# Windowed attention in front of two expert layers: the plain heads' value shift moved from a VectorE copy to a DMA inside SBUF, and half of the other value copies put on ScalarE

## The chip, the core and the metric

One core of one Trainium2 chip runs the whole program. It has TensorE (PE), VectorE (DVE), ScalarE (ACT), GpSimd (POOL), and SyncE (SP), which here only issues transfers. SP, ScalarE and GpSimd each have a queue of transfers, all of which run on the core's 16 DMA engines. The metric is the time of one execution on the device, in microseconds (us); less is better. L12 is line 12 of the kernel.

## The reference

Attention over 4 batches of 8 heads, 576 positions of 64 numbers each; a position sees the 32 positions up to its own (heads 0 to 3, "plain") or every fourth of the last 128 (heads 4 to 7, "dilated"). Its output goes through a layer that sends each of 2304 tokens to one of 8 experts, and then through a second layer.

```python
scores = scale * np.matmul(q, k.transpose(0, 1, 3, 2))
mask_plain = (rel >= 0) & (rel < 32)
mask_dil = (rel >= 0) & (rel < 128) & (rel % 4 == 0)
attn = exp(scores - max) / (sum + 1e-09)       # masked, h < 4 plain, else dilated
x = np.matmul(attn, v)                         # then tokens x 512
idx = np.argmax(xn @ en.T / tau, axis=1)       # expert of each token
y[e] = gate * (np.maximum(x[e] @ w1[e], 0) @ w2[e])
out = (h - np.tanh(h)) @ w_out                 # h = y @ w_in
```

## The kernel before

The first 180 us or so are the attention and the choice of experts; the expert layer and the last layer follow, and the change doesn't touch these two.

**Units and turns.** The attention is cut into 19 units (`units`), numbered 0 to 18. A unit is ("d", b, c) for half of the dilated heads of batch b, ("p", b, c) for half of the rows of the plain heads, ("l", 0, c) and ("t", 0, 0) for the rests of 576 positions that don't fill 128 rows. Units 9 and 11 are plain ones of batch 2, units 14 and 17 plain ones of batch 3, units 15 and 16 are "l". The order is written out by hand and each engine runs it in order. Turn n of the loop does, one after the other:

- `plan[n]`: transfers that are issued ahead, nearly all on SP (`load`, L420);
- `scores(n + 2)` on TensorE, and between its halves the transposes of the keys and queries of unit n + 3 (L550); then `softmax(n + 2)`: VectorE takes the maximum `mx` (L666) and subtracts it into `sm` (L669), ScalarE makes the exponentials `pr` (L674);
- `mid[n]`;
- `values(n)` on TensorE (L722), and after it the transposes of the probabilities of unit n + 1, copied out by ScalarE as `pT` (L685); VectorE divides the result (L731 to L742);
- `after[n]`.

The scores lie in one PSUM buffer (`sc`), so TensorE can't begin the scores of unit n + 3 (L631) before `sm` of unit n + 2 has read it. `mid` and `after` hold the extra work: `route_norm`, `route_low`, `route_transpose` (a transposing transfer on SP, L919), `route_choice` (TensorE's products L953, then small operations), `route_place`, which build the expert choice group by group of tokens, and the value copies below.

**Values.** A block of 32 queries needs the values of its own 32 keys and of the 32 before, on 64 partitions for each of two heads. For the plain heads `load_vp(b, par)` brings the own blocks into partitions 32 to 63 (par 0) or 96 to 127 (par 1) of `vwp[b % 2]`, and `shift_vp(b, par)` copies them one block further into the 32 partitions below, which makes them "the block before". It runs in `after` of turns 0 and 1 (batch 0), 2 and 3, 6 and 7, 10 and 11 (batch 3), eight times in all. For the dilated heads `expand_v` copies pieces of 32 partitions into `vwd` and `vwl`, through `vcopy`, which gives every VP-th copy to ScalarE and the others to VectorE.

**Semaphores of transfers.** The transfers that SP and ScalarE issue take eight semaphores, DMAHW0 to DMAHW7, in turn in the program's order, whichever of the two issues them. Each waits before it is issued until the last transfer that took its own semaphore has landed. SP's queue is issued in order.

Of the kernel before, what the change touches and what calls it, by code (L numbers as in the profile page):

```python
# [49 lines left out]
T0 = R0 * KAPPA - T1 * T1  # L50
BURST = 10
NST = 6
VP = 3


@with_exitstack
def kernel(
# [18 lines left out]
    nc = tc.nc  # L76
# [317 lines left out]
    with ExitStack() as actx:  # L394
# [18 lines left out]
        def four(src, b, h0, i0, n):  # L413
            return src[b, h0:h0 + 4, 4 * i0:4 * i0 + 4 * n, :].rearrange("h (i c) d -> i h (c d)", c=4)
# [53 lines left out]
        vwp = [tp.tile([128, 18, 2, D + 1], F32, tag=f"vwp{i}", name=f"vwp{i}", bufs=1) for i in range(2)]  # L468
# [32 lines left out]
        def shift_vp(b, par):  # L501

            p0 = 64 * par
            nc.vector.tensor_copy(out=vwp[b % 2][p0:p0 + 32, 1:18], in_=vwp[b % 2][p0 + 32:p0 + 64, 0:17])

        ncopy = [0]

        def vcopy(o, i):
            ncopy[0] += 1
            (nc.scalar.copy if ncopy[0] % VP == 0 else nc.vector.tensor_copy)(out=o, in_=i)  # L510

# [588 lines left out]
        for b in range(B):  # L1100
            plan[max(at["p", b, 0] - 1, 0)].append((room_x, (b,)))
            plan[(3, 7, 11, 14)[b]].append((load_x, (b,)))
            if b:
                for g in range(4):
                    after[4 * b - 4 + (3 * g) // 3].append((expand_v, (b, g)))
            for par in range(2):
                after[(0, 2, 6, 10)[b] + par].append((shift_vp, (b, par)))
            after[at["p", b, 0]].append((keep_vt, (b,)))
# [31 lines left out]
        for c in range(2):  # L1140
            for nm, src, eng in (("k", k, nc.sync), ("q", q, nc.scalar)):
                eng.dma_start(
                    out=raw["d", nm, 0][:, :, 128 * c:128 * c + 128],
                    in_=four(src, 0, 4, 0, 128)[:, :, 128 * c:128 * c + 128],
# [93 lines left out]
    for x in x2l[::-1] + x2h[::-1]:  # L1238
# [10 lines left out]
        out=key, in0=ncnt[0:1, :], scalar=float(E), in1=later, op0=ALU.mult, op1=ALU.add  # L1249
    )  # L1250
    nc.vector.scalar_tensor_tensor(
        out=key, in0=is_first, scalar=float(E * (NT + 1)), in1=key, op0=ALU.mult, op1=ALU.add
# [3 lines left out]
        out=ahead, in0=key.unsqueeze(1).to_broadcast(sh), in1=key.unsqueeze(2).to_broadcast(sh), op=ALU.is_gt  # L1256
# [6 lines left out]
        out=at_place, in0=rank.unsqueeze(1).to_broadcast(sh), in1=order.unsqueeze(2).to_broadcast(sh), op=ALU.is_equal  # L1263
# [4 lines left out]
        out=picked[:, 0:E], in0=at_place, in1=order.unsqueeze(1).to_broadcast(sh), op=ALU.mult  # L1268
# [8 lines left out]
        out=before, in0=rank.unsqueeze(1).to_broadcast(sh), in1=order.unsqueeze(2).to_broadcast(sh), op=ALU.is_lt  # L1277
# [11 lines left out]
        out=zf[:, 0:E], in0=sums[:, 0:E], scalar=float(XS), in1=pn, op0=ALU.mult, op1=ALU.add  # L1289
    )  # L1290
    nc.vector.scalar_tensor_tensor(
        out=zf[:, E:2 * E], in0=pn, scalar=-16.0, in1=caps, op0=ALU.add, op1=ALU.is_lt
    )
    nc.vector.scalar_tensor_tensor(
        out=zf[:, 2 * E:], in0=zf[:, 0:E], scalar=-float(E * XS), in1=zf[:, E:2 * E], op0=ALU.add, op1=ALU.mult
# [8 lines left out]
        out=mine, in0=rank.unsqueeze(2).to_broadcast(sh), in1=order.unsqueeze(1).to_broadcast(sh), op=ALU.is_equal  # L1304
# [465 lines left out]
```

## Time and profile before

| what | value |
|---|---|
| runs shown | 784.86, 784.91, 788.17 us; median 784.91 |
| profiled execution | 786.13 us; span from first to last instruction 784.5 us |
| mean granted clock of TensorE | 0.948 |
| busy over the span | PE 92%, DVE 62%, ACT 49%, POOL 26% |

The span is what the views of the trace count from; 1.6 us of the profiled execution lie outside it. A wait in brackets, as [1.28 <-DVE vwp L504], is the idle time of the engine before the instruction and what ended it. PEclk of 1.00 is the full clock of TensorE, 0.50 half of it. A chain of work that ended last can be followed back only to 172 us in this trace, so in the attention the waits are read engine by engine.

### The profile page before, as it was taken

Reading aid. Unit: us, or ns where it says so; the run is one execution under the profiler, and the core shown is the slowest. Engines: PE = TensorE matmul, PEld = TensorE weight load, DVE = VectorE, ACT = ScalarE, POOL = GpSimd, SP = SyncE. Lnnn points to the kernel's source line nnn. Section 1 sums busy time; section 2 is a strip of 40 time slices with the busy share of each in tenths; the row PEclk is TensorE's granted clock in tenths of the full one; section 3 lists DMA queues with packets and bytes.
Section 4 is the critical chain, followed back from the end, with each engine's and each line's share of the span. In section 5 each row is a group of like instructions: output and inputs, shape, how many; then the busy total and the mean of one; then the engine's idle time right before and its main releaser. Section 6 shows DMA issues by size and latency. Waiting matters only on the chain.

```text
span 784.5 us, 16969 instructions
## 1 busy us (share of the span) xinstructions
PE 718.1 (92%) x6773; PEld 451.9 (58%) x6773; DVE 486.3 (62%) x1019; ACT 381.5 (49%) x812; POOL 200.3 (26%) x244
## 2 busy tenths in 40 slices
PE   8787898538999999999997999999999999999994
PEld 5666676425666666788854555555555555555541
DVE  4788597585777777989869997333334343424420
ACT  4565547333655656777556565332423332423401
POOL 2155526375000000000003221412321322322311
PEclk9998698658999999999999999999999999999998
DMA  9869757749988868998600410100100100100001
GB/s 225 176 165 220 167 130 170 217 178 291 256 246 241 252 215 204 276 268 257 230 29 28 109 54 1 41 1 1 41 0 1 41 1 1 41 0 1 22 22 43
DMA packets 115828, 95.33 MB, mean 122 GB/s; under 512 B 72187, under 2 KB 99099, under 8 KB 115739
## 3 DMA queue, kind: packets, MB, share of 16 engines
q1 hardware_dynamic: 109083, 77.12, 36.9%
q0 software_dynamic: 5312, 16.40, 6.3%
q8 instruction: 55, 0.90, 0.5%
q10 hardware_dynamic: 1344, 0.62, 0.3%
q14 instruction: 34, 0.28, 0.1%
HBM read 67.12 MB, written 18.26 MB: 109 GB/s over the span
## 4 chain that ended last, share of the span: by engine, by line
PE 63%; DVE 5%; issue 4%; ACT 3%; POOL 1%; DMA 1%; POOLq 0%; SPq 0%; ACTq 0%; DVEq 0%
PE hp L1543 21%; PE po L1599 20%; PE y L1368 11%; PE ph L1348 10%; DVE w2l L187 1%; ACT w2h L177 1%; ACT sq L1406 1%; DVE c L1585 1%; POOL out L1608 1%; DMA xTe<-xs 1%; ACT u L1553 0%; DVE c L1563 0%; ACT U L1575 0%; POOL gl L1581 0%; DVE y L1427 0%
## 5 line engine op out<-in xcount | busy, mean ns | idle before, releaser
L1556 DVE CUSTOM_DVE_ANT_0 U<-u,sig 128x384 f32<-128x384 f32 x96 | 52.1, 580 | 161.2 <-ACT u L1553 161.2
L1581 POOL TENSOR_TENSOR gl<-c,gh 128x768 f16<-128x768 f32 x48 | 83.0, 1730 | 259.5 <-ACT gh L1580 259.5
L1553 ACT ACTIVATE u<-hp 128x384 f32<-128x384 f32 x96 | 46.0, 485 | 176.2 <-PE hp L1543 169.0
L1543 PE MATMUL hp<-x2h,win_h 128*128 128x384 f16 x384 | 125.2, 326 | 5.7 <-DVE c L1563 4.4
L1543 PE MATMUL hp<-x2h,win_l 128*128 128x384 f16 x384 | 125.2, 326 | 0.0
L1543 PE MATMUL hp<-x2l,win_h 128*128 128x384 f16 x384 | 124.0, 326 | 0.0
L1348 PE MATMUL ph<-xTe,w1h 128*128 128x352 f16 (+6 forms) x512 | 102.7, 294 | 10.3 <-DMA xTe<-xs 8.3
L1543 PEld LDWEIGHTS <-win_h 128*128 128x128 f16 x768 | 75.1, 98 | 59.5 <-DVE c L1563 7.6
L1599 PE MATMUL po<-wo_l,gh 128*128 128x512 f16 x288 | 109.2, 379 | 0.0
L1599 PE MATMUL po<-wo_h,gl 128*128 128x512 f16 x288 | 109.2, 379 | 0.0
L1599 PE MATMUL po<-wo_h,gh 128*128 128x512 f16 x288 | 109.1, 379 | 0.0
L1599 PEld LDWEIGHTS <-gh 128*128 128x128 f16 x576 | 56.3, 98 | 64.5 <-issue 1.0
L1348 PE MATMUL ph<-xTe,w1l 128*128 128x352 f16 (+6 forms) x256 | 75.3, 294 | 0.0
L1368 PE MATMUL y<-hh,w2h 128*128 128x352 f16 (+6 forms) x256 | 74.7, 292 | 0.0
L1368 PE MATMUL y<-hh,w2l 128*128 128x352 f16 (+6 forms) x256 | 74.6, 291 | 0.0
L1368 PE MATMUL y<-hl,w2h 128*128 128x352 f16 (+6 forms) x256 | 74.6, 291 | 0.0
L1348 PEld LDWEIGHTS <-w1h 128*128 128x128 f16 x512 | 50.5, 99 | 25.3 <-issue 9.2
L1368 PEld LDWEIGHTS <-w2h 128*128 128x128 f16 x512 | 50.1, 98 | 17.2 <-issue 0.8
L1585 DVE SCALAR_TENSOR_TENSOR c<-U,c 128x768 f32<-128x768 f32 x48 | 45.9, 957 | 11.2 <-ACT U L1575 11.2
L1543 PEld LDWEIGHTS <-win_l 128*128 128x128 f16 x384 | 37.6, 98 | 26.4
L1448 POOL DMA_DIRECT2D row_d<-rw x8 | 4.3, 534 | 174.0 <-ACT rw L1447 174.0
L1599 PEld LDWEIGHTS <-gl 128*128 128x128 f16 x288 | 28.2, 98 | 34.0
(278 smaller groups left out, 1251.7 us busy)
## 6 DMA issues: line engine op xcount, KB each, us to landing
wst<-in_moe_w SPq DMA_DIRECT2D x64, 512.0 KB, 7.6
wst<-in_moe_w_in SPq DMA_DIRECT2D x16, 512.0 KB, 5.6
wst<-in_moe_w_out SPq DMA_DIRECT2D x16, 512.0 KB, 3.6
vwp<-in_v SPq DMA_DIRECT2D x16, 144.0 KB, 6.2
rv<-in_v SPq DMA_DIRECT2D x4, 512.0 KB
rk<-in_k SPq DMA_DIRECT2D x16, 128.0 KB, 3.5
rq<-in_q SPq DMA_DIRECT2D x16, 128.0 KB, 5.2
xp<-xd_d SPq DMA_DIRECT2D x4, 512.0 KB, 4.2
```

What stands on the lines that cost most here:

```text
L177: nc.scalar.activation(out=hi, in_=st, func=ACTF.Copy, scale=SW)
L187: nc.vector.scalar_tensor_tensor(out=lo, in0=st, scalar=SW, in1=hi, op0=ALU.mult, op1=ALU.subtract)
L1348: nc.tensor.matmul(ph[:, 0:CAPS[e]], lhsT=wt[e, f // 2][w][:, c:c + 128], rhs=xT[:, a + d, 0:CAPS[e]], start=(i == 0), stop=(i == 11), ski ...
L1368: nc.tensor.matmul(y[dc][:, 0:CAPS[e]], lhsT=w[:, c:c + 128], rhs=h[:, f, 0:CAPS[e]], start=(f == 0 and i == 0), stop=(f == 7 and i == 2), ...
L1406: nc.scalar.activation(out=st["sq"][:, dc, 0:n], in_=y[dc][:, 0:n], func=ACTF.Square)
L1543: early(b, "x2", nc.tensor.matmul(hp[:, a, 0:NB], lhsT=w[d][:, 128 * f:128 * f + 128], rhs=x[d][:, c0:c0 + NB], start=(w is win_h and x is ...
L1553: nc.scalar.activation(out=u[:, a], in_=hv[:, a], func=ACTF.Square, accum_out=usum[:, n:n + 1])
L1556: early(b, "sg", nc.vector.tensor_tensor_reduce(out=U[:, a], in0=u[:, a], in1=sig2[:, c0:c0 + NB], scale=1.0, scalar=0.0, op0=ALU.mult, op ...
L1581: nc.gpsimd.tensor_tensor(out=gl, in0=tc_, in1=gh, op=ALU.subtract)
L1585: nc.vector.scalar_tensor_tensor(out=c, in0=U, scalar=T0, in1=c, op0=ALU.add, op1=ALU.mult)
L1599: nc.tensor.matmul(po[t][:], lhsT=g[:, a, 128 * t:128 * t + 128], rhs=w, start=(f == 0 and i == 0), stop=(f == 15 and i == 2), skip_group_ ...
L1608: i = nc.gpsimd.indirect_dma_start(out=out, out_offset=bass.IndirectOffsetOnAxis(ap=tok["id"][:, T:T + 1], axis=0), in_=o[:], in_offset=No ...
```

## The change

`shift_vp` issues a DMA on ScalarE's queue from SBUF to SBUF, for the same 32 partitions of 2210 numbers (8840 bytes each), in place of a copy on VectorE. VP goes from 3 to 2, so that of the 88 value copies of `vcopy` 44 are on ScalarE, before 29.

```diff
-VP = 3
+VP = 2
...
         def shift_vp(b, par):
 
             p0 = 64 * par
-            nc.vector.tensor_copy(out=vwp[b % 2][p0:p0 + 32, 1:18], in_=vwp[b % 2][p0 + 32:p0 + 64, 0:17])
+            nc.scalar.dma_start(out=vwp[b % 2][p0:p0 + 32, 1:18], in_=vwp[b % 2][p0 + 32:p0 + 64, 0:17])
```

On VectorE, in `after` of turn 6 (b is 2, par is 0): after the division of unit 6 stand three copies and the shift, ahead of the maximum of unit 9.

```order
 L742 TENSOR_TENSOR xd<-xo,rr 128x512
-L510 COPY vwd_103<-rv 32x8x64 x3
-L504 COPY vwp_99<-vwp_99 32x2210
+L510 COPY vwd_103<-rv 32x8x64 x2
 L666 TENSOR_REDUCE mx<-sc 128x8
 L669 TENSOR_TENSOR sm<-sc,mx 128x2x4x64
```

One copy and the shift are gone from there.

On ScalarE, in `after` of turns 10 and 11 (b is 3), the program after the change. A bracket names the semaphores for which the instruction waits; `kTl` is the key copy of unit 15.

```order
L510 COPY vwd_104<-rv 32x8x64 x2
L504 DMA vwp_100<-vwp_100 32x2210 [waits DMAHW3_49,DMAHW2_49,DMAHW1_49]
L560 COPY kTp<-tr 128x2x2x128 [waits PE_49]
L577 COPY qT<-tr 128x512 [waits PE_49]
L674 ACTIVATE pr<-sm 128x512 [waits DVE_49]
L685 COPY pT<-pt 128x512 [waits PE_49]
L510 COPY vwd_104<-rv 32x8x64 x2
L510 COPY vwl<-rv 32x8x64
L504 DMA vwp_100<-vwp_100 32x2210 [waits DMAHW5_49,DMAHW6_49,DMAHW2_49,DMAHW0_49]
L564 COPY kTl_108<-tr 128x4x4x32 [waits PE_49]
```

Before, there stood one copy of `vwd` ahead of `kTp` and two ahead of `kTl`, and no DMA.

On SP, the transfers of turns 9 and 10, first before the change (`vwp_100` is batch 3's, `xT` the transposing transfers of the second group of tokens, `lk` and `lq` the keys and queries of units 15 and 16):

```order
L420 DMA vwp_100<-in_v 32x18x64 [waits DMAHW2_49,PE_49]
L420 DMA vwp_100<-in_v 32x18x64 [waits DMAHW3_49,PE_49]
L919 DMA_TRANSPOSE xT<-xg 128x8x128 [waits DMAHW4_49,PE_49,Pool_49]
L919 DMA_TRANSPOSE xT<-xg 128x8x128 [waits DMAHW5_49,Pool_49]
L420 DMA lk<-in_k 16x4x256 [waits DMAHW6_49,Activation_49]
```

The same place after the change, and on to the last of `lq`. The two numbers that are left out in the turn of eight, DMAHW1 between the two `vwp_100` and DMAHW5 behind the two `xT`, are taken by ScalarE's shifts of batch 3, par 0 and par 1.

```order
L420 DMA vwp_100<-in_v 32x18x64 [waits DMAHW0_49,PE_49]
L420 DMA vwp_100<-in_v 32x18x64 [waits DMAHW2_49,PE_49]
L919 DMA_TRANSPOSE xT<-xg 128x8x128 [waits DMAHW3_49,PE_49,Pool_49]
L919 DMA_TRANSPOSE xT<-xg 128x8x128 [waits DMAHW4_49,Pool_49]
L420 DMA lk<-in_k 16x4x256 [waits DMAHW6_49,Activation_49]
L420 DMA lk<-in_k 16x4x256 [waits DMAHW7_49]
L420 DMA lk<-in_k 16x4x256 [waits DMAHW0_49]
L420 DMA lk<-in_k 16x4x256 [waits DMAHW1_49]
L420 DMA lq<-in_q 16x4x256 [waits DMAHW2_49]
L420 DMA lq<-in_q 16x4x256 [waits DMAHW3_49]
L420 DMA lq<-in_q 16x4x256 [waits DMAHW4_49]
L420 DMA lq<-in_q 16x4x256 [waits DMAHW5_49]
```

The instructions of SP are the same in the same order; the fourth `lk` now waits on the semaphore of the shift of par 0 and the fourth `lq` on that of par 1, where both waited before on transfers of SP itself.

## Rows read from the trace of the kernel before

**Rows 1.** Windows: busy us per engine (PE PEld DVE ACT POOL), then PEclk, DMA share, GB/s.
```profile
20.00:120.00 100.00, 84.50 (x2165) 66.06 (x2160) 80.19 (x183) 54.59 (x107) 40.61 (x59) 0.86 0.77 173
70.00:88.00 18.00, 18.00 (x359) 14.25 (x357) 12.51 (x39) 10.12 (x21) 4.56 (x8) 0.53 0.89 217
```

**Rows 2.** Timeline of TensorE: start us, us, form, in brackets the wait before.
```profile
31.68 0.93 PE L550 MATMUL tr<-id,rq 128*128 128x128 f32 x4 [2.40 <-DMA rq<-in_q]
...
45.80 0.57 PE L631 MATMUL xo<-mask_sb,idm 128*128 128x240 f16 x4 [1.28 <-DVE vwp L504]
...
54.65 0.58 PE L631 MATMUL sc<-mask_sb,idm 128*128 128x240 f16 x4 [1.14 <-DVE sm L669]
...
61.85 0.59 PE L631 MATMUL sc<-mask_sb,idm 128*128 128x240 f16 x4 [2.06 <-DVE sm L669]
...
69.32 0.58 PE L631 MATMUL sc<-mask_sb,idm 128*128 128x240 f16 x4 [2.44 <-DVE sm L669]
...
86.89 0.96 PE L631 MATMUL sc<-mask_sb,idm 128*128 128x240 f16 x4
...
105.26 0.59 PE L631 MATMUL sc<-mask_sb,idm 128*128 128x240 f16 x4 [1.06 <-DVE sm L669]
...
107.02 0.66 PE L550 MATMUL tr<-id,lq 128*128 128x128 f32 x4
...
110.13 1.35 PE L953 MATMUL rps<-en,xT 128*128 128x8 f16 x48
111.35 0.57 PE L631 MATMUL sc<-mask_sb,idm 128*128 128x240 f16 x4
```

**Rows 3.** Source views of L504 and L510: durations ns min/median/max.
```profile
L504 DVE COPY vwp<-vwp x8: 1293/1302/2148, 23.1 to 107.9; 32x2210 f32<-32x2210 f32 x8
...
L510 DVE COPY vwd<-rv x47: 281/417/3403, 12.3 to 106.7; 32x512 f32<-32x512 f32 x28, 32x256 f32<-32x256 f32 x19
L510 ACT COPY vwd<-rv x23: 400/615/622, 12.9 to 107.0; 32x512 f32<-32x512 f32 x14, 32x256 f32<-32x256 f32 x9
```

**Rows 4.** Timeline of VectorE: turns 4 and 6.
```profile
49.24 3.83 DVE L510 COPY vwd<-rv 32x512 f32<-32x512 f32 x2
...
63.13 2.56 DVE L510 COPY vwd<-rv 32x512 f32<-32x512 f32 x3
65.72 2.15 DVE L504 COPY vwp<-vwp 32x2210 f32<-32x2210 f32 x1
```

**Rows 5.** Timeline of ScalarE: turns 11 and 13.
```profile
105.77 0.57 ACT L685 COPY pT<-pt 128x512 f32<-128x512 f32 x1
106.37 1.26 ACT L510 COPY vwd<-rv 32x512 f32<-32x512 f32 x2
...
116.95 0.61 ACT L876 ACTIVATE jq<-xp 128x512 bf16<-128x512 f32 x1
```

**Rows 6.** Timeline of SP's queue: loads and transposing transfers of turns 10 to 11.
```profile
92.92 2.69 SPq L420 DMA_DIRECT2D lq<-in_q  x4
95.65 1.93 SPq L420 DMA_DIRECT2D lv<-in_v  x4
99.37 3.37 SPq L919 DMA_TRANSPOSE xT<-xg  x2
...
109.45 0.54 SPq L698 DMA_DIRECT2D xp<-xd_d  x1
```

**Rows 7.** DMA issues by line: KB each, median us to landing.
```profile
vwp<-in_v SPq DMA_DIRECT2D x16, 144.0 KB, 6.2
...
xp<-xd_d SPq DMA_DIRECT2D x4, 512.0 KB, 4.2
...
lq<-in_q SPq DMA_DIRECT2D x4, 64.0 KB, 4.8
...
xt<-xl_d SPq DMA_DIRECT2D x2, 128.0 KB, 2.6
```

**Rows 8.** View of the tile xT: landing of SP's transposing transfers.
```profile
DMA to landing us min/median/max: 3.1/3.9/4.7
```

## The prediction

> **What bounds the kernel now.** The time of the profiled execution is 786.13 us (span 784.5), 1.2 above the median of 784.91; a difference worked out in its trace is added to the median. The stages behind 180 us aren't touched and start when the attention is done, so I ask by how much the attention's end moves. I read first the windows [rows 1]: from 20 to 120 us TensorE is busy 84.5 of 100, VectorE 80.2, ScalarE 54.6. TensorE and VectorE take turns being late, and ScalarE has room. Then TensorE's timeline for its waits [rows 2]. It waits for VectorE 1.28 us in turn 4, 1.14 at the start of turn 6 (54.65), 2.06 at turn 7, 2.44 at turn 8 (69.32) and 1.06 at turn 12 (105.26). In turn 4 the shift itself is named; in the others `sm`, which stands behind copies on VectorE. The reader should see also that TensorE's clock falls after the 2.44 wait: from 70 to 88 us the granted clock is 0.53 [rows 1], nearly its lower level of 1.2 GHz, and TensorE is busy all of it. Turns 8 and 9 last from 69.32 to 86.89, 17.6 us. Turn 12 does the same as turn 8 at full clock in 6.1 us (105.26 to 111.35), 1.2 of it the products L953 that turn 9 lacks [rows 2].
>
> **What the change takes from VectorE.** Eight shifts of 1.3 us, the longest 2.15 [rows 3], and 15 value copies of 0.42. Only what TensorE waits for counts:
>
> - Turn 4: the shift is gone. 1.3.
> - Turn 6: ahead of `mx` stand two copies of 3.83 us together [rows 4], of which the longest is 3.4 [rows 3]. One goes to ScalarE, and if the one that stays takes the usual 0.42, the wait of 1.14 goes: 1.1. If it takes 3.4, 0.4 is left.
> - Turn 7: the two copies ahead stay on VectorE and the whole chain just starts sooner. 0.
> - Turn 8: one of three copies (2.56 / 3 = 0.85) and the shift of 2.15 go [rows 4], 3.0 against a wait of 2.44: 2.4.
> - Turns 8 and 9 at full clock, if the wait that comes before the low clock is gone: 6.1 + 4.9 + 0.3 for small products = 11.3 in place of 17.6, so 6.3. I take off 1.5, because TensorE then comes 5 us sooner to where `xp` is used, and that is read back from DRAM (4.2 us to landing [rows 7]) only once `xd` has been written there. 4.8, with 0 and 6.3 as the bounds.
> - Turn 12: 1.1 for `sm`, and ScalarE is that much sooner; this one I book below.
>
> Up to turn 12 that is 1.3 + 1.1 + 2.4 + 4.8 = 9.6 us.
>
> **What it puts on ScalarE and the DMA engines.** A copy that moves takes 0.62 on ScalarE (0.40 for the half-size ones of the start, against 0.28) [rows 3], 9 us in all in an engine that is idle for 45%. At the start, where it isn't, some 1.2 us may be lost before turn 2, but there TensorE waits 2.40 us for `rq` anyway (31.68) [rows 2], which covers it; without that cover it costs 1.2. The issue of a transfer takes about 0.5 on its queue (four of `lv`: 1.93) [rows 6]. The trace has no transfer from SBUF to SBUF. For its landing the nearest rows are `xt`, 128 KB on a quiet queue, 2.6 us, and `vwp`, 144 KB in short pieces on a full one, 6.2 [rows 7]; the shift is 276 KB in 32 long pieces. I take 3.0, nearer `xt` as the queue will be quiet (below), with 2.6 and 6.2 as bounds. The readers of the shift have a turn or more, except in turn 2, which waits for `rq` until 31.68 in any case.
>
> The Trainium skill, in "DMA: Bandwidth & Descriptors", section "Anatomy of one DMA — SWDGE (gpsimd) path", fits 2.0 us plus the bytes at 436 GB/s; that would be an estimate of 2.65 us, though its fit is for another issuing path. By it the sum below comes out 0.35 us lower.
>
> **What the new waits do.** This is the part that decides. The shift isn't only a transfer, it takes a semaphore out of the turn of eight, and SP's queue stands until it has landed. Six of the eight shifts are waited for by transfers that SP issues later than the shift lands, or whose readers have a turn to spare (the third `rq` of turn 1 is needed in turn 4). The last two aren't. In the trace SP issues `lk` and `lq` until 95.6 us [rows 6], whereas ScalarE comes to the shift of turn 11 only behind `pT` at 105.77 [rows 5]. So the fourth `lq`, and all of SP's queue behind it, goes from 95 us to after that shift. TensorE needs `lq` at 107.02 [rows 2].
>
> In the clock of the trace of before: `pT` 105.77, less the 1.1 of turn 12, and 0.57 long, ends at 105.2; three copies of 0.62, 107.1; issue, 107.6; landing after 3.0, 110.7. Then SP issues `lq` (0.5; landing 2.6 as `xt` to 4.8 as `lq` before [rows 7], I take 3.0): TensorE can go on at 113.7, not at 107.0. Behind `lq` stand `lv` (1.9) and the two transposing transfers `xT` (3.4) [rows 6]; the second begins at 114.8 and lands 3.9 later [rows 8], at 118.7. TensorE needs it for L953, at 110.13 before [rows 2], and comes there from 113.7 in 3.1 us at full clock or about 5.8 at half, 116.8 to 119.5. I take 119, 8.9 us late. Then `xp`: SP ends `xT` at 116.5 and needs 6.7 more until its issue (102.74 to 109.45) [rows 6], so 123.2; it lands 4.2 later [rows 7], at 127.4. ScalarE wants it 6.8 after L953 (116.95) [rows 5], at 125.8, and stands 1.6 with `pT` behind it, of which I count 1.0, as TensorE has its own work until `pT` is needed. With 0.5 for a low clock after TensorE's idle time the loss is 10.4 us. At the shortest landings (2.6 for the shift, `lq` and `xp`, 3.1 for `xT`) it is about 8; at the longest (6.2, 4.8, 4.7) about 15.
>
> The Trainium skill says in the same section that DMA engines don't wait on semaphores, and that any such wait is spent on the issuing sequencer before dispatch. By that rule SP stands, and all of its queue with it, for a transfer that the next ones don't need. The trace agrees: SP goes on to `lv`, `xT` and `xp` only in order [rows 6].
>
> **Sum.** 10.4 lost and 9.6 gained: 0.8 slower, 784.9 + 0.8 = 785.7, and I say 786 us.
>
> **The rivals.**
>
> 1. The low clock of turns 8 and 9 isn't avoided but only moved: TensorE still idles nearly 2 us at turn 7, and the 4.8 aren't gained. Then 10.4 - 4.8 = 5.6 slower, 790.5. For it speaks that the clock falls elsewhere in the attention too (0.86 on average from 20 to 120 [rows 1]); against it, that the wait of 2.44 right ahead of it, the longest of the five, is one of those that go. A landing of the shift of 6 us in place of 3 comes to about half of that and adds to it. It decides where turns 8 and 9 give back less than 1.7 us, since 10.4 - 4.8 - 1.7 is 3.9.
> 2. The loads land at their shortest and turns 8 and 9 run at full clock without the 1.5 that I took off: 8 lost against 11.1, 3.1 faster, 782. It decides over 0.5% once another 0.8 us is gained. Against it: in order, the fourth `lq` can't be issued before the shift has landed, and TensorE is in order too.
> 3. The naive reading, that SP doesn't wait and only VectorE's work goes: 9.6 + 1.1, 774. The rows of SP in the changed program speak against it.
> 4. ScalarE becomes the bound: 9 us of copies and 8 issues come ahead of `pr` and `pT`. If half of the copies showed on the path, 4.5 us on top of the forecast, 790. Against it: it is idle for 45% of the stretch [rows 1], and its copies stand where it waits for VectorE or TensorE next.
>
> **How the numbers follow.** Forecast (within 0.5%, which is 3.9 us and about what a measurement of this kernel can tell from no change) 0.47; rival 1, with long landings, 0.24; rival 2 0.18, half of it beyond 0.5%; rival 3 0.03; rival 4 0.08. Faster by over 0.5%: 0.09 + 0.03 = 0.12. Slower: 0.24 + 0.08 = 0.32. The rest 0.56. The range reaches from a little below rival 2 to a little above rivals 1 and 4, 780.5 to 792.5; rival 3 and the longest landings are left out.
>
> **What would show it.** In the profile of the changed kernel: TensorE's waits for `sm` at turns 6 and 8 and for the shift in turn 4 gone; turns 8 and 9 in about 12 us at a granted clock near 1.00 (if they take 17 again, rival 1); turn 12's transposes of `lq` with a wait of 6 to 9 us that a DMA ends, and a second wait of 1 to 3 at L953 for `xT`; SP with a gap of some 8 us ahead of its fourth `lq`; issue to landing of the shift near 3 us. If TensorE doesn't wait for `lq`, my reading of the semaphores is wrong and the kernel is faster; if ScalarE's copies stand ahead of late `pr`, it is rival 4.

## The result, and the profile after

The changed kernel takes 798.69 us (median of 20 runs, 791.02 to 802.78), the kernel before in the same session 787.40 (20 runs, 782.02 to 795.87). The ratio is 1.0141, 95% interval 1.0115 to 1.0167: slower by 1.4%, some 11 us. The forecast was 786, no change, with a range from 780.5 to 792.5. The profiled execution of the changed kernel took 792.37 us (span 790.7) and lies at the low end of its runs, that of before near its median; so the two traces show only 6.2 of the 11 us, and what they show is tested below on kernels with one part of the change. The mean granted clock of TensorE in the profiled execution of the changed kernel is 0.950, the highest of its 20 runs; their median is 0.933, where the kernel before has 0.945 to 0.946 in the three later sessions. So most executions of the changed kernel have a lower clock than the trace that is read here.

The windows of the changed kernel, columns as in [rows 1], the third one added:

```profile
20.00:120.00 100.00, 81.72 (x2085) 64.40 (x2071) 58.99 (x153) 58.76 (x112) 34.72 (x57) 0.84 0.88 190
70.00:88.00 18.00, 16.23 (x437) 12.95 (x435) 12.38 (x42) 10.96 (x22) 3.32 (x8) 0.91 1.06 238
106.00:124.00 18.00, 18.00 (x373) 14.15 (x371) 10.16 (x39) 7.18 (x15) 1.56 (x3) 0.56 0.55 125
```

VectorE is relieved by 21 us of 100 (80.19 to 58.99), and TensorE has less done, not more (84.50 to 81.72 busy). The low clock of 70 to 88 us, 0.53, near half of the full clock, isn't in this trace (0.91). But it stands from 106 to 124, at 0.56, where in the trace of before it was 0.94 (experiment 12, without the change, has 0.94 and 0.70 in these two stretches):

```profile
106.00:124.00 18.00, 16.22 (x466) 12.57 (x464) 15.15 (x48) 11.70 (x23) 5.24 (x9) 0.94 0.48 142
```

TensorE's timeline of the changed kernel, the places of [rows 2] (the starts of turns 3, 6 to 8 and 10 to 14, and the waits):

```profile
33.70 1.15 PE L550 MATMUL tr<-id,rq 128*128 128x128 f32 x4 [4.43 <-DMA rq<-in_q]
39.09 0.92 PE L631 MATMUL sc<-mask_sb,idm 128*128 128x240 f16 x4
...
55.47 0.57 PE L631 MATMUL sc<-mask_sb,idm 128*128 128x240 f16 x4
63.70 0.98 PE L631 MATMUL sc<-mask_sb,idm 128*128 128x240 f16 x4 [2.86 <-DVE sm L669]
70.09 0.57 PE L631 MATMUL sc<-mask_sb,idm 128*128 128x240 f16 x4
...
85.11 0.57 PE L631 MATMUL sc<-mask_sb,idm 128*128 128x240 f16 x4
91.14 0.57 PE L631 MATMUL sc<-mask_sb,idm 128*128 128x240 f16 x4
99.57 1.01 PE L631 MATMUL sc<-mask_sb,idm 128*128 128x240 f16 x4
105.59 1.09 PE L550 MATMUL tr<-id,lq 128*128 128x128 f32 x4 [3.40 <-DMA lq<-in_q]
112.25 0.96 PE L631 MATMUL sc<-mask_sb,idm 128*128 128x240 f16 x4
121.06 0.87 PE L631 MATMUL sc<-mask_sb,idm 128*128 128x240 f16 x4
```

The same places in the trace of before that [rows 2] doesn't have, the starts of turns 3 and 14:

```profile
36.42 0.66 PE L631 MATMUL sc<-mask_sb,idm 128*128 128x240 f16 x4
...
116.41 0.57 PE L631 MATMUL sc<-mask_sb,idm 128*128 128x240 f16 x4
```

Trace against trace this reads: turn 3 starts 2.7 later, because the wait for `rq` grew from 2.40 to 4.43 and ends at 33.70 in place of 31.68. By turn 6 (54.65 before) the lag is 0.8; turn 12 starts 5.7 sooner (105.26). There the predicted wait for `lq` stands, 3.40 us long, and turn 13 starts 0.9 later than before. Turn 13 at half clock lasts 8.8 us in place of 5.1, so turn 14 is 4.6 late, and the attention ends 4 to 5 late. Experiment 12 shows that the trace of before is itself late at turn 12, so the differences in the middle can't be put down to the change.

SP's queue of the changed kernel, answering [rows 6], with the start of the program ahead:

```profile
25.64 1.55 SPq L760 DMA_DIRECT2D cst_sb<-const_cst  x1
...
28.57 5.55 SPq L420 DMA_DIRECT2D rq<-in_q  x4
...
91.69 5.54 SPq L420 DMA_DIRECT2D lk<-in_k  x4
97.28 6.24 SPq L420 DMA_DIRECT2D lq<-in_q  x4
103.56 1.93 SPq L420 DMA_DIRECT2D lv<-in_v  x4
105.59 2.62 SPq L919 DMA_TRANSPOSE xT<-xg  x2
```

and the same places of the kernel before that [rows 6] doesn't have:

```profile
24.74 1.31 SPq L760 DMA_DIRECT2D cst_sb<-const_cst  x1
...
27.43 2.05 SPq L420 DMA_DIRECT2D rq<-in_q  x4
...
90.94 1.94 SPq L420 DMA_DIRECT2D lk<-in_k  x4
```

The four `lq` take 6.24 us of SP's queue in place of 2.69, and four `rq` 5.55 in place of 2.05. SP's waits in the stretch 18 to 125 us name the shift (us in all, times, the longest):

```profile
SPq L420 <- DMA vwp<-vwp: 6.2, 3, 3.3
```

So SP stands for three shifts: 1.2 us in `rq`, the rest in `lk` and `lq`, the longest ahead of the fourth `lq`. The other 2.3 us that the four `rq` take more are issues that last longer.

### The profile page after: what moved, and what is told of

Same layout as the page of the kernel before. It is cut to its first block, busy times and chain, and to the rows that moved or that the text cites. A ratio compares the mean times of both kernels' runs of the same rounds, so it can differ in the third digit from the quotient of the medians.

```text
span 790.7 us, 16971 instructions
## 1 busy us (share of the span) xinstructions
PE 717.4 (91%) x6773; PEld 451.7 (57%) x6773; DVE 465.2 (59%) x996; ACT 390.9 (49%) x827; POOL 195.9 (25%) x244
## 4 chain that ended last, share of the span: by engine, by line
PE 59%; DVE 6%; issue 5%; ACT 3%; DMA 3%; POOL 1%; POOLq 0%; ACTq 0%; SPq 0%; DVEq 0%
PE hp L1543 21%; PE po L1599 20%; PE ph L1348 9%; PE y L1368 8%; DMA wst<-in_moe_w 2%; DVE w2l L187 1%; ACT w2h L177 1%; DVE c L1585 1%; POOL out L1608 1%; DMA xTe<-xs 1%; DVE hl L1357 1%; DVE y L1427 1%; ACT u L1553 0%; DVE c L1563 0%; ACT sq L1406 0%
```

## The experiments

Each was timed against the kernel before in the same session (medians of before: 783.39 us for experiments 1 to 4, 784.14 for 5 to 8, 783.26 for 9 to 12). Differences of ratios are turned into us with 785.

**1. The copies alone** (`VP = 2`, the shift stays on VectorE).

```diff
-VP = 3
+VP = 2
```

> VP of 2 alone, the shift stays a copy on VectorE. Three theories of the 11 us that the change lost. S: SP's queue stands for the last two shifts, by the semaphores that they take. C: the copies load ScalarE, so that pr and pT come late. D: the transfers of the first shifts delay the loads of the start. S and D: within 3 us of before or up to 3 faster, as 15 copies leave VectorE and no transfer is new. C: 4 to 11 us slower than before.

783.05 us, ratio 0.9989 (0.9964 to 1.0013). No change. The copies cost nothing and bring nothing.

**2. The transfer alone** (the shift by DMA, VP stays 3).

```diff
-            nc.vector.tensor_copy(out=vwp[...][p0:p0 + 32, 1:18], in_=vwp[...][p0 + 32:p0 + 64, 0:17])
+            nc.scalar.dma_start(out=vwp[...][p0:p0 + 32, 1:18], in_=vwp[...][p0 + 32:p0 + 64, 0:17])
```

> The shift as a DMA alone, VP of 3. S and D: 8 to 12 us slower than before, the whole loss of the change, with SP standing ahead of the fourth lk and the fourth lq, and TensorE waiting 3 us or more for lq. C: within 3 us of before.

794.12 us, 1.0131 (1.0094 to 1.0168): the whole loss is the transfer's. Its profiled execution is near its median, so its trace shows the loss at full size. TensorE's timeline of this kernel, turns 3 and 12 and what follows them:

```profile
40.76 1.01 PE L631 MATMUL sc<-mask_sb,idm 128*128 128x240 f16 x4
...
102.58 0.57 PE L631 MATMUL sc<-mask_sb,idm 128*128 128x240 f16 x4
107.52 1.08 PE L550 MATMUL tr<-id,lk 128*128 128x128 f32 x4 [4.14 <-DMA lk<-in_k]
...
117.63 0.96 PE L631 MATMUL sc<-mask_sb,idm 128*128 128x240 f16 x4
```

4.3 late at turn 3, 2.7 early at turn 12, 6.3 late at turn 13. The shift's landing in the same kernel (its source view) is 5.3 in the median, not 3.0:

```profile
DMA to landing us min/median/max: 4.0/5.3/8.4
```

**3. The last two shifts back on VectorE** (the changed kernel otherwise).

```diff
+            if b == 3:
+                nc.vector.tensor_copy(...)
+                return
             nc.scalar.dma_start(...)
```

> The change with batch 3's two shifts back on VectorE; the six others stay DMAs. S: lk and lq are issued by 97 us again, TensorE doesn't wait for lq, and most of the loss goes: 7 to 11 us faster than the change, about the time of before or up to 3 less. D: the wait for rq at about 30 us stays over 4 us, and no more than 5 us come back. C: no more than 2 come back, those of the two shifts.

788.02 us, 1.0058 (1.0033 to 1.0082). The last two shifts are worth 1.0141 - 1.0058 = 0.83%, 6.5 us; 0.6% stays with the first six, which no theory of mine had at that size.

**4. A tiny transfer at the places of the last two shifts** (the kernel before, with two transfers of 2 KB on ScalarE's queue besides).

```diff
+            if b == 3:
+                nc.scalar.dma_start(out=tiny[par][:, 1], in_=tiny[par][:, 0])
```

> The kernel before, with the shift on VectorE and VP of 3, and two DMAs of 2 KB between two tiny tiles added on ScalarE's queue where batch 3's shifts stand; they move nothing that anyone reads, but they take semaphores, and the second lk and the second lq wait for them. S: 6 to 11 us slower than before, though no transfer or copy of note is added. C and D: within 2 us of before.

786.01 us, 1.0034 (1.0007 to 1.0062): 2.7 us, less than half of what I had expected, though SP stands 5.8 us in the four `lk` (7.75 in place of 1.94). SP's queue and TensorE's waits of this kernel:

```profile
89.22 7.75 SPq L420 DMA_DIRECT2D lk<-in_k  x4
```

```profile
99.11 1.08 PE L555 MATMUL tr<-id,lk 128*128 128x128 f32 x4 [2.82 <-DMA lk<-in_k]
102.39 1.08 PE L555 MATMUL tr<-id,lq 128*128 128x128 f32 x4 [1.19 <-DMA lq<-in_q]
```

So the stand exists with no work moved and hardly a byte. It is a matter of where in the program a transfer takes its semaphore.

**5. Only the middle four by DMA** (batches 1 and 2; batches 0 and 3 on VectorE, VP = 2).

```diff
+            if b in (0, 3):
+                nc.vector.tensor_copy(...)
+                return
             nc.scalar.dma_start(...)
```

> Shifts of batches 1 and 2 by DMA, those of batches 0 and 3 back on VectorE, VP 2. Known so far: all eight by DMA 794 beside 783.4 for the kernel before, the last two back on VectorE 788. Theory S+T (S: SP's queue stands for the last two shifts by the semaphores; T: at the start the bytes of the first two shifts crowd the DMA engines and hold up SP's issues of rq): both places are taken away, the first wait for rq is about 2.4 again at 31.7, and what VectorE saves in turns 4 to 8 shows: 776 to 781. Rival M (what the middle shifts save comes back later, since the low clock and the later waits only move): 782 to 785. Rival N (the middle shifts themselves cost): 786 to 789.

783.99 us, 0.9991 (0.9970 to 1.0012; one of its 12 executions, of 2512.7 us, is left out of the ratio): no loss, and no gain either. With experiment 3 the first two shifts are worth 1.0058 - 0.9991 = 0.67%, 5.3 us, and the middle four nothing. TensorE's timeline of this kernel (its lines are numbered 3 higher), the starts of turns 12 and 13 and the wait between:

```profile
95.89 0.58 PE L634 MATMUL sc<-mask_sb,idm 128*128 128x240 f16 x4
...
106.52 0.48 PE L956 MATMUL rps<-en,xT 128*128 128x8 f16 x12 [3.42 <-DMA xT<-xg]
106.86 0.96 PE L634 MATMUL sc<-mask_sb,idm 128*128 128x240 f16 x4
```

Turn 12 starts 9.4 us sooner than in the trace of before (105.26), and the forecast had said 9.6; but experiment 12 shows the same with every shift on VectorE. Then TensorE stands 3.42 for `xT`, and turn 13 starts only 4.5 sooner (111.35); the profiled span is 1.3 shorter, the median not at all.

**6. The shifts on GpSimd's queue**, which takes none of the eight semaphores.

```diff
-            nc.scalar.dma_start(...)
+            nc.gpsimd.dma_start(...)
```

> All eight shifts by DMA, but issued on GpSimd's queue, whose transfers take other semaphores, so that SP never waits for a shift. Theory S alone: no loss left, 776 to 780. S+T: the stand for the last two goes, but the bytes of the first two still crowd the start: first wait for rq again above 4 us, SP without a stand ahead of lk and lq: 780 to 786. Without S (the transfers cost, not the semaphores): 792 to 795.

791.82 us, 1.0099 (1.0067 to 1.0131). A miss: without any stand of SP for a shift most of the loss is still there. TensorE's waits for transfers in this kernel:

```profile
37.82 0.66 PE L722 MATMUL xo<-vwp,pT 64*32 64x65 f32 x30 [1.86 <-DMA vwp<-vwp]
...
116.87 0.48 PE L953 MATMUL rps<-en,xT 128*128 128x8 f16 x12 [5.05 <-DMA xT<-xg]
```

The shift of turn 1 now comes too late for its own readers, as GpSimd gets to it only at 30.65 us; and two shifts go out at 106.7 and 107.2, together with `xT`, whose landing takes up to 10.2 us (tile view of `xT`, 88 to 119 us; before, the longest was 4.7 [rows 8]):

```profile
DMA to landing us min/median/max: 3.7/7.0/10.2
```

**7. A tiny transfer at the places of the first two shifts** (as 4, with `if b == 0`).

> The kernel before with two further 2 KB transfers on ScalarE's queue at the places of the first two shifts: the semaphores are taken, no bytes move and no shift leaves VectorE. T (bytes): nothing changes, 782.5 to 784.5, wait for rq in turn 2 near 2.4. S at the start (semaphores): rq late by 1 to 3, 785 to 787.

785.15 us, 1.0013 (0.9993 to 1.0032): no change that can be told, against 0.67% for the shifts themselves. But it isn't the clean case that I expected. The time lies in the range that was set for the semaphores, SP stands 2.8 us for one of the two transfers, and TensorE's wait for `rq` isn't near 2.4:

```profile
32.93 1.24 PE L555 MATMUL tr<-id,rq 128*128 128x128 f32 x4 [4.16 <-DMA rq<-in_q]
```

Turn 3 starts at 38.41, 2.0 later than in the trace of before. So a wait of that length in one trace isn't by itself a loss that the runs show.

**8. `lk`, `lq` and `lv` issued two turns earlier** in the changed kernel.

```diff
-            (9, load_p, (3, "q")), (9, load_vp, (3, 1)), (10, load_l, ()), (11, load_t, ()),
+            (9, load_p, (3, "q")), (9, load_vp, (3, 1)), (8, load_l, ()), (11, load_t, ()),
```

> The changed kernel with the loads of lk, lq and lv put two turns earlier in the program, so that lk and lq take their semaphores ahead of batch 3's shifts; nothing else is moved. S: PE's wait of 3 to 4 us for lq or lk in turn 12 goes, 785 to 789 as with the last two shifts on VectorE. Without S (the last two transfers cost by themselves): 792 to 796.

792.72 us, 1.0115 (1.0081 to 1.0149). A miss, but not against the stand. SP's queue of this kernel, and TensorE's wait:

```profile
90.65 9.82 SPq L420 DMA_DIRECT2D lv<-in_v  x4
```

```profile
103.22 1.36 PE L550 MATMUL tr<-id,rq 128*128 128x128 f32 x4 [5.59 <-DMA rq<-in_q]
```

With `lk` and `lq` out of the way SP stands in `lv` (9.82 us for 1.93), and now `rq` of unit 14 is behind it, issued from 100.56 on. The stand only moved to another reader, so this kernel doesn't show what the last two transfers cost without it.

**9 to 12. The same transfer besides.** The kernel before, with its shifts on VectorE, and at the places of two shifts the same 276 KB moved into a tile that nobody reads: nothing is taken from VectorE and nobody waits for the data. On ScalarE's queue it takes a semaphore, on GpSimd's it doesn't.

```diff
+        mock = tp.tile([128, 17, 2, D + 1], F32, name="mock", bufs=1)
...
             nc.vector.tensor_copy(...)
+            if b == 0:
+                nc.scalar.dma_start(out=mock[p0:p0 + 32], in_=vwp[b % 2][p0 + 32:p0 + 64, 0:17])
```

> The kernel before, its shifts all on VectorE, and at the places of batch 0's two shifts the same transfer besides, on ScalarE's queue, into a tile that nobody reads (276 KB each, semaphores taken). Known: batch 0's two shifts by DMA cost 4 us (all but the last two by DMA 788.0, only the middle four 784.0), two tiny transfers here 1.0. Theory B (bytes: the transfer itself crowds the DMA engines at the start, and SP's loads of rq issue and land later): 786 to 789, rq of turn 2 about 2 late. Theory S (only the semaphores hold SP up): like the tiny ones, 784 to 786. Theory W (the cost is the wait of the shift's own readers): 783 to 784.5.

> The same two transfers besides, on GpSimd's queue: bytes as before, none of the semaphores that SP waits on. B: 786 to 789 as on ScalarE's queue. S: no change, 783 to 784.5.

> The kernel before and at the places of batch 3's two shifts the same transfers besides on ScalarE's queue, read by nobody. Known: the last two shifts by DMA cost 6.5 us, two tiny transfers in their place 2.7. S with the true length of the landing (SP stands until 3 to 8 us after the issue, so lk, lq, xT and xp all go later than with tiny ones): 787 to 791. If it stays at the 2.7 of the tiny ones, the rest is the wait of the shift's own readers or what VectorE does otherwise: 785.5 to 787.

> The same two transfers besides on GpSimd's queue: bytes without the stand of SP. S: no change or up to 1, 783 to 785. B (bytes delay lq and xT on full DMA engines): 786 to 790, with a later landing of xT.

| two transfers besides | on ScalarE's queue | on GpSimd's | 2 KB on ScalarE's |
|---|---|---|---|
| batch 0's places | 1.0045 (1.0027 to 1.0063) | 1.0055 (1.0027 to 1.0083) | 1.0013 (0.9993 to 1.0032) |
| batch 3's places | 1.0064 (1.0038 to 1.0089) | 1.0018 (0.9998 to 1.0037) | 1.0034 (1.0007 to 1.0062) |

At the start two full transfers cost on either queue, on GpSimd's with no semaphore that SP waits for, so the loss needs none; two tiny ones can't be told from nothing. (On ScalarE's queue the full and the tiny ones are 0.32% apart, hardly more than the 0.27% to which that difference is known.) At the end a transfer on ScalarE's queue costs, one on GpSimd's can't be told from nothing; but GpSimd came to its two only at 102.0 us, ScalarE at 87.9 and 93.8, so the places aren't quite the same.

The start of the kernel of experiment 10, where SP doesn't wait for any of the two: SP's queue, then TensorE.

```profile
25.65 2.06 SPq L763 DMA_DIRECT2D cst_sb<-const_cst  x1
...
29.09 4.04 SPq L420 DMA_DIRECT2D rq<-in_q  x4
```

```profile
35.39 0.69 PE L553 MATMUL tr<-id,rq 128*128 128x128 f32 x2 [5.09 <-DMA rq<-in_q]
```

SP's issues themselves take longer (`cst_sb` 2.06 in place of 1.31, four `rq` 4.04 in place of 2.05), and TensorE goes on 3.7 later (31.68 before). The end of the kernel of experiment 11: SP's queue, SP's waits, TensorE.

```profile
87.25 7.45 SPq L420 DMA_DIRECT2D lk<-in_k  x4
```

```profile
SPq L420 <- DMA mock<-vwp: 6.3, 2, 5.3
```

```profile
98.77 1.08 PE L553 MATMUL tr<-id,lk 128*128 128x128 f32 x4 [4.47 <-DMA lk<-in_k]
```

Experiment 12 shows one thing more. Its work is that of the kernel before until its two transfers go out at 102.0 us, and its time can't be told from that of before. TensorE's timeline of it, the starts of turns 8, 10, 12 and 13 and the wait ahead of 13:

```profile
71.08 0.98 PE L634 MATMUL sc<-mask_sb,idm 128*128 128x240 f16 x4
...
82.79 0.59 PE L634 MATMUL sc<-mask_sb,idm 128*128 128x240 f16 x4
...
95.99 0.57 PE L634 MATMUL sc<-mask_sb,idm 128*128 128x240 f16 x4
...
105.02 0.46 PE L956 MATMUL rps<-en,xT 128*128 128x8 f16 x12 [1.17 <-DMA xT<-xg]
105.33 0.57 PE L634 MATMUL sc<-mask_sb,idm 128*128 128x240 f16 x4
```

With nothing taken off VectorE, turns 8 and 9 last 11.7 us, at a granted clock of 0.94 from 70 to 88 us, and turn 12 starts 9.3 us sooner than in the trace of before. From turn 3 to turn 12 the traces of experiments 4, 7, 10, 11 and 12, all with the shifts on VectorE and `VP` 3, take 58 to 59 us (9 takes 63), experiment 5 59.8, the changed kernel 60.5. The trace of before takes 68.8: it is the one that stands apart, by its low clock in turns 8 and 9 and a slow turn 10. Why it had them no run here shows.

## Why the prediction was wrong

**What held.** SP stands until the last two shifts have landed, and TensorE waits for `lq` in turn 12. In the changed kernel L953 begins at 110.93; the forecast, with its gain taken off, had 119 - 9.6 = 109.4. That these come so near is luck: the wait for `lq` was 3.40 and not 6 to 9, there was none for `xT`, where 1 to 3 had been forecast, and SP's gap ahead of the fourth `lq` was 3.3 and not 8. The waits of turns 6 and 8 and that for the shift in turn 4 are gone (turn 4 has one of 0.85 for `mx` instead, and that of turn 7 grew, 2.06 to 2.86). Rivals 2 (faster) and 3 (SP doesn't wait) are out. So is rival 4: the copies alone change nothing (experiment 1).

**The step that failed first: the start was costed at nothing.** The prediction let the wait of 2.40 for `rq` cover what the first two shifts do, and priced a transfer by its own landing and by who reads it. But that wait is a transfer's, on the same 16 DMA engines, and it isn't a fixed time: two transfers of 276 KB go out at 21.6 and 27.8 us, SP's issues take longer, and in the changed kernel the wait is 4.43. Turn 3 is 2.7 us late there, in experiment 2 4.3; over many runs the first two shifts cost 0.67% (experiment 3 against 5). The same transfers with no reader cost 0.55% on GpSimd's queue, where SP waits for neither (10), and 0.45% on ScalarE's (9). That the loss comes by way of `rq` is read from the traces and not shown: experiment 7 has nearly the same wait, 4.16, and no loss that can be told. The Trainium skill states in "DMA: Bandwidth & Descriptors", section "Issuing engines are not separate DMA queues", that whichever engine starts a transfer, it runs on the same 16 DMA engines and interleaves with the others. Experiments 9 and 10 agree, 1.0045 and 1.0055.

**The second: "up to turn 12 that is 9.6" was read off one execution, and added to the sum as if it reached the end.** Against the trace of before its size seems about right (9.4 in experiment 5; 8.4 from turn 3 to turn 12 in the changed kernel), but that is luck: experiment 12 is 9.3 sooner with all its shifts on VectorE. Half of the forecast, the 4.8 of turns 8 and 9, was to come from a low clock that the kernel before needn't have. The parts don't fit either: in the changed kernel turns 8 and 9 give 2.6 in place of 4.8, and turn 10 gives 4.3 that weren't forecast. And a gain ahead of turn 13 is held up at `xT`. In before, SP's second issue of `xT` starts at about 101.5 and lands 3.1 to 4.7 later [rows 6, 8], so that TensorE, at L953 at 110.13, could have come only some 4 to 5.5 us sooner before it would wait, as long as `xT` itself came no sooner. This could have been read. What is left of it behind turn 13 (4.5 in experiment 5's trace, 6.0 in experiment 12's) isn't in the time of the runs of either.

**The third: the low clock of turns 8 and 9 was booked as saved.** TensorE's granted clock from 20 to 132 us (the last number but two), before and changed kernel:

```profile
20.00:132.00 112.00, 94.56 (x2372) 73.49 (x2366) 88.30 (x205) 62.90 (x124) 50.08 (x74) 0.85 0.77 175
```

```profile
20.00:132.00 112.00, 91.12 (x2249) 71.37 (x2235) 65.31 (x173) 67.39 (x130) 43.51 (x72) 0.83 0.86 191
```

The 4.8 us of turns 8 and 9 were to come from full clock. In the 14 traces the mean over this stretch lies between 0.79 and 0.85 (experiment 1 has 0.80, 5 has 0.85); the low part is in each of them, at different places. In the changed kernel it stands behind the new wait, and turn 13 lasts 8.8 us in place of 5.1, where I had booked 0.5. But turn 13 lasts 8.0 to 8.8 in experiments 1, 5 and 12 too, which lose nothing, so this isn't what the change lost. Rival 1, which I gave 0.24, named such a move; its own sign, that turns 8 and 9 give back less than 1.7, didn't come (2.6 in the trace).

The runs say more of the clock than the traces. The share of the clock that is missing, times the span, is 51.9 us on average over the 20 runs of the changed kernel and 41.8 to 42.7 for the kernel before in the later sessions. By this estimate up to some 9 of the 11 us go with a lower clock. How much of that the waits at the start and in turn 12 bring isn't shown.

**The loss of the last two was over-sized**, 10.4 against 6.5 (experiment 3). The term that was mis-sized is TensorE's wait for `lq`, 6.7 in the sum (113.7 less 107.0) and 3.40 in the changed kernel. With the gain of 9.6 taken off, `lq` was to be there at 104.1 and came at 105.6; TensorE was to be there at 97.4 and came at 102.2. So `lq` came 1.5 us later than forecast and TensorE, late from the start and without the gain, 4.8 later, and it had only the rest of the delay to wait for. The landing is 5.3 in the median of experiment 2, not 3.0, but the last one in the changed kernel, the one that counts, took some 3.2. (The working also counts the shift's issue of 0.5 beside its landing, which the views count from the issue on.)

**The sum, mended** (by the experiments): first two shifts +5.3, middle four and copies -0.7, last two +6.5, together the measured 11. (They are steps between the ratios of experiments 5, 3 and the changed kernel, and so add up in any case; each of the two large ones is known to about 0.35% either way.) What of the 6.5 is the stand and what the bytes stays open: two tiny transfers cost 2.7 and two full ones 5.0, with intervals that overlap, the test with `lk` and `lq` out of the way (8) moved the stand, and the one without any stand (6) costs 0.99% by waits of its own.

## What to carry to other kernels

A transfer that takes work off a busy engine is to be priced at three places: its bytes against the loads that are in flight then, the semaphore that it takes out of a shared turn (which later transfer waits for it, and what stands behind that one in its queue), and only then its own readers. A wait for a DMA is no cover for more DMA traffic. A gain that rests on a stretch of low clock in one trace is no price until a second execution shows the same stretch. And before adding any gain in the middle to the sum, read how long ahead of its use each later transfer lands.

## What was not expected of the hardware

- The same transfer of 276 KB within SBUF (32 rows of 8840 bytes) lands after 4.0 to 8.4 us (experiment 2), and beside the loads of the start after 6.4 to 6.8 on ScalarE's queue and 6.4 to 6.7 on GpSimd's (9 and 10). The Trainium skill's fit in "DMA: Bandwidth & Descriptors", section "Anatomy of one DMA — SWDGE (gpsimd) path", gives an estimate of 2.65; the measurement decides.
- The issue of a small transfer on SP's queue isn't a fixed price: 44 KB of `cst_sb` took 1.31 us in before, 1.55 in the changed kernel, 2.06 in experiment 10, with SP waiting for nothing that the profile names.
- One wait of 3.4 us in turn 12 was followed by a stretch at a granted clock of 0.56 over 18 us, in which TensorE was busy all the time; experiment 12, with waits of 1.44 and 1.17 in turn 12, has 0.70 there.
